# Tile 5's first layer by seven block products, a shorter x ring and another order of the work in a fused attention and MLP kernel

## The chip, the cores and the metric

The kernel runs on one core of one Trainium2 chip. The metric is the device time of one execution in microseconds (us); a kernel's time is the median of its runs. Below, PE is TensorE (matrix products), PEld its weight loads, DVE is VectorE, ACT is ScalarE, POOL is GpSimd and SP is SyncE, which issues most transfers.

## What is computed

Eight batches of attention with eight heads, 576 rows and 64 columns per head, in a form without a score matrix, and behind it a two-layer network on all 4608 rows:

```python
q_s = softmax(q, over the 64 columns)
k_s = softmax(k, over the 576 rows)
kv  = einsum('bhsd,bhse->bhde', k_s, v)
x   = einsum('bhsd,bhde->bhse', q_s, kv)     # becomes 4608 rows of 512
h   = x @ w_in                               # 512 -> 2048
g   = maximum(0.01 * h, h)
out = g @ w_out                              # 2048 -> 512
```

Inputs and output are 32-bit floats; the products are made of bf16 operands with 32-bit sums.

## The kernel before

**Attention, by batch.** `load` (line 76) brings q, k or v of one batch into one of six buffers of the pool `raw` (line 61), 1152 KB each. For k, the maximum over the rows is taken by a tree on DVE (`k_tree`, line 147: nine row groups, first four against four, then two against two, one against one, and the ninth), carried across partitions (`k_allmax`, line 162), subtracted (`k_sub`) and exponentiated on ACT (`k_exp`). For q, DVE takes maxima (`q_max`, line 222), POOL subtracts them, ACT exponentiates, DVE sums (`q_sum`) and normalises (`q_norm`), all in place of the loaded buffer or in `qe`. `q_turn` (line 454) sends the normalised q through a transposing transfer issued by SP; its result is `qX`. For batches 1 and 2 this is done in two halves, of five and of four row groups. PE makes k^T v (`kv_half`, line 288) and, in `quads` (line 433), x transposed in PSUM, named `po`; `move` (line 427) copies it into `xT`, a ring of columns (token) with the four blocks of 128 features. The ring has `NX = 4 * S` = 2304 columns (line 54).

**The network, by tile.** 4608 tokens are nine tiles of 512. In tile 0 both layers are plain. From tile 1 on the second layer is made by seven block products of a 2x2 block scheme instead of eight (`behind`, line 930, words "P"): sums and differences of g are made on DVE (line 1008, words "n") and those of w_out beforehand (`wsums`). The first layer comes in two forms:

- plain (`layer1`, line 511, words "u"): for each of the 16 feature blocks four products of 512 columns into one PSUM bank, then a leaky eviction on ACT (line 525, words "l");
- by seven block products (`ahead`, line 902, words "m"): for one quarter of the features 7 x 4 products of 256 columns; three partial sums per quarter are copied out by ACT (line 985, words "s1", "s5", "s6") into `part_spare`, three sums are made by DVE (line 989, by `total`, line 900, words "c11", "c22", "c12"), and four leaky evictions follow, three of which read from `part_spare`. It needs sums of x (`xsums`, words "X") and of w_in (`fsums`, words "F"), and buffers for partial sums, which are taken from the pool `raw` (words "Z").

Tiles 1 to 4 have the plain form, tiles 6, 7 and 8 the block form, and tile 5 the plain form for three quarters of the features and the block form for the fourth.

**What sets the order.** Each engine works through its own instructions in program order. Up to tile 0 that order is given by calls and by hooks (`at`). From tile 1 to the end of tile 6 it is the list of words `SCORE` (line 803); for tiles 7 and 8 it is `WEAVE` (line 845). A word issues all instructions of one step on whatever engines it uses. A digit ahead is the tile; "u13" is the second half's feature block 3. Of the words without a tile, "lq3" loads q of batch 3 (SP), "kt3.0" to "kt3.3" are steps of the tree, "km3" the maximum across partitions, "qm3" q's row maximum, "qt2.0" and "qt2.1" the transposing transfers, "A2.0" to "A2.2" the quads, "x2.01" a move on ACT. "d11" to "d22" add a kept partial sum (words "q1", "q5", "q6") to a PSUM bank into the output buffer (line 1027) and thereby empty that bank, "w" issues the stores.

Of the kernel before, what the change touches and what calls it, by code (L numbers as in the profile page):

```python
# [8 lines left out]
FP32 = mybir.dt.float32  # L9
# [16 lines left out]
def kernel(  # L26
# [9 lines left out]
    nc = tc.nc  # L36
# [3 lines left out]
    B, H, S, D = q.shape  # L40
# [22 lines left out]
    qe_pool = ctx.enter_context(tc.tile_pool(name="qe", bufs=1))  # L63
    mx_pool = ctx.enter_context(tc.tile_pool(name="mx", bufs=1))
# [82 lines left out]
    def k_tree(b, hs, steps=slice(0, 4)):  # L147
        n = hs.stop - hs.start
        ks = st[b]["k"][:, hs]
        if steps.start == 0:  # L150
            st[b]["t4"] = mx_pool.tile([P, HL, 4, D], FP32, name="t4")[:, 0:n]
        t4 = st[b]["t4"]
        t2, t1 = t4[:, :, 0:2], t4[:, :, 0]
        for o, i0, i1 in (
            (t4, ks[:, :, 0:4], ks[:, :, 4:8]),
            (t2, t2, t4[:, :, 2:4]),
            (t1, t1, t4[:, :, 1]),
            (st[b]["kmax"][:, hs], t1, ks[:, :, 8]),
        )[steps]:
            nc.vector.tensor_tensor(out=o, in0=i0, in1=i1, op=ALU.max)  # L160

# [265 lines left out]
    def move(eng, o, i):  # L427
        if eng is nc.scalar:
            eng.copy(out=o, in_=i)  # L429
        else:  # L430
            eng.tensor_copy(out=o, in_=i)
# [14 lines left out]
    def attend(b, gg, c0, n, engs, pool=psB_pool, tag=BANK_TAG):  # L446

        ps = [pool.tile([P, n], FP32, name="po", tag=tag) for _ in range(2)]
        qT = st[b]["qT", gg]
        quads(b, gg, ps, lambda hh: qT[:, hh].rearrange("c r l -> c (r l)")[:, c0 : c0 + n])  # L450
        for hp in range(2):
            move(engs[hp], xT[:, 2 * gg + hp, b % 4 * S + c0 : b % 4 * S + c0 + n], ps[hp])

    def q_turn(b, rs=ALLR):
        if "qX" not in st[b]:
# [3 lines left out]
            in_=st[b]["qe"][:, rs].rearrange("p r h d -> p (r h d)"),  # L459
        )  # L460

    def attend_made(b, i, g0, per):
        qX = st[b]["qX"].rearrange("c (r g) (h l) -> c g h r l", g=2, h=2)
        rs = XR[i]
        n = (rs.stop - rs.start) * L
        cols = slice(b % 4 * S + rs.start * L, b % 4 * S + rs.stop * L)
# [9 lines left out]
        return [(xT[:, 2 * g0 + hp : 2 * g0 + hp + 2 * per - 1 : 2, cols], ps[hp]) for hp in range(2)]  # L476

    def attend_joint(b, i):
        qX = st[b]["qX"].rearrange("c (r g) (h l) -> c g h r l", g=2, h=2)
# [7 lines left out]
        for gg in ggs:  # L487
# [7 lines left out]
        c0 = b % 4 * S + rs.start * L  # L495
        g0 = ggs[0]
        return [
            (xT[:, 2 * g0 + hp : 2 * ggs[-1] + hp + 1 : 2, c0 : c0 + n], ps[hp]) for hp in range(2)
        ]

    def attend_x(b, parts, engs):

        made = []
        for i in parts:
            per = 512 // ((XR[i].stop - XR[i].start) * L)
            for g0 in range(0, 2, per):
# [283 lines left out]
    def xsums(t, steps=slice(0, 4)):  # L790
# [10 lines left out]
            nc.vector.tensor_tensor(out=o, in0=x, in1=y, op=op)  # L801

    SCORE = """
        1u13 1u02 kt2.1 kt2.2 kt2.3 1u00 qm2.1 qm2.0 lq3 1u03 1l02 1l03 1l13 1l00 1u01 1u06 1u04 1l01 1u17
        qs2.1 qe2.1 1l06 km2 1l04 qu2.1 qs2.0 1l17 1u05 qe2.0 ks2 1u10 qu2.0 1u07 qn2.0 1P100 1l05 1u11 1l10
        lk3 qt2.0 1u12 1u16 va2 1l11 1l07 1u14 ksB2 1l16 1u15 1P101 1P110 1l12 1n0_0 1P200 1l14 1l15 1P201
        1P210 1P211 1P111 1n0_1 qn2.1 1n1_1 1P500 1P501 vb2 ke2 1q1 1P510 1n1_0 1d11 kv2 1P511 1q5 kr2 kd2
        1P600 1P601 1P610 1P611 qt2.1 1n3_0 lq4 1n3_1 1n2_1 1P300 lv3 1n2_0 1P301 A2.0 A2.1 A2.2 1q6 x2.01
        T3 kt3.0 kt3.1 x2.11 kt3.2 1P310 1P311 kt3.3 qm3 x2.20 1P700 1P701 1P710 1P711 x2.21 x2.00 x2.10
        2u11 2u00 2l00 2u01 2l01 2l11 2u10 2l10 va3 2u04 1d22 1P400 1P401 1P410 1P411 vb3 1d12 qm4 2u05 2l04  # L810
        qs3 qe3 2u14 2l14 2u02 2u06 2u12 lk5 2l05 2u13 2l02 2l06 2l12 km3 2u07 2u16 2u03 qu3 qn3 2l07 2l13
        2u17 1q21 2l03 2u15 2l15 2P100 ks3 ksB3 2n0_0 2l17 qs4 2P101 2P110 2P111 2P200 2l16 2P201 2P210
        2P211 2P500 2n0_1 2n1_0 2n1_1 2P501 2P510 lk4 kt4.0 lq5 ke3 kv3 kr3 2q1 2d11 2n2_0 1w0 2P600 qt3
        2P601 lv6 2P610 2P611 2P511 kd3 A3.0 kt4.1 2n2_1 2n3_0 kt4.2 2n3_1 A3.1 2q6 kt4.3 2q5 A3.2 2P700
        2P701 2P710 x3.01 2P711 x3.11 2d22 x3.10 2P300 x3.20 2P301 2P310 x3.21 qe4 km4 ks4 ksB4 kt5.0 lv4
        2P311 x3.00 2P400 va4 2P401 2P410 kt5.1 3u02 3l02 2P411 3u03 3u00 vb4 3l00 kt5.2 kt5.3 3u01 3l01 km5
        3l03 ke4 3u11 3l11 3u06 3u04 3l04 3u16 2q21 3l06 3l16 3u12 3l12 3u14 3u10 3l10 lk6 ks5 qu4 3u15 3l15
        kv4 3l14 kr4 kd4 3u07 2d12 qn4 3u05 3u13 3u17 3P100 3l05 3l07 3P101 3P110 3P111 lk7 3l13 3n0_0 3P500
        lv5 3l17 3n0_1 3P501 3P510 3q1 ke5 3n1_0 3n1_1 3n3_0 3P511 3P600 3n3_1 3q5 3P601 va5 3P610 3P611 3q6
        1w1 3P300 3P301 3P310 vb5 3P311 kt6.0 3n2_0 qt4 A4.0 A4.1 A4.2 kv5 x4.01 kt6.1 3n2_1 x4.00 x4.21  # L820
        x4.10 2w0 va6 3P700 kt6.2 kt6.3 3P701 3P710 qm5 qs5 3P711 3P200 3P201 x4.11 3P210 3P211 x4.20 kr5
        kd5 3d22 vb6 4u02 4l02 3P400 3P401 3d11 3P410 4u04 4u00 qe5 4l00 3P411 km6 4l04 4u05 4l05 3q21 4u03
        4u14 4l14 4l03 4u10 4l10 4u06 lv7 4u07 4u11 4l11 4u01 4l01 4l06 3d12 4l07 qu5 qn5 ks6 kt7.0 3w0 4u12
        4l12 4u13 F3 4l13 F1 4P100 4P101 4P110 F2 ke6 4u15 4P111 4q1 4n0_0 4l15 4u17 4l17 kt7.1 4n1_0 4u16
        3w1 4P500 4l16 4n0_1 4n2_0 qt5 A5.0 A5.1 x5.01 x5.10 x5.00 A5.2 kv6 x5.20 kt7.2 2w1 x5.11 4P501
        4P510 4n1_1 4P511 4q5 x5.21 4n3_0 4P600 4n3_1 4P200 4P601 4P610 4n2_1 X5.0 4P300 4P611 lq6 X5.1 X5.2
        4P201 4P301 4P310 4q6 X5.3 4P700 4P701 5u00 va7 kt7.3 4P210 F4 vb7 4P710 4P711 qm6 qs6 4d22 lq7 kr6
        4P211 4d11 5u04 4P311 kd6 4P400 4P401 5l00 4P410 5u02 km7 4P411 5l04 5u05 4q21 5l05 5l02 qm7 qe6 qu6
        5u15 5l15 5u11 5l11 ks7 Z0 5u03 5m5_3 5u12 5m1_3 5s1_3 5m2_3 5c11_3 qs7 4d12 5u01 5l12 5l03 5m6_3
        5u10 5s5_3 5m3_3 5s6_3 5c12_3 5l11_3 5m7_3 5u13 5l01 5P100 5P101 5c22_3 5l22_3 5m4_3 5l10 5l13 5u14  # L830
# [208 lines left out]
    def of_batch(word):  # L1039
# [108 lines left out]
```

## Time and profile before

| what | value |
|---|---|
| median of 3 runs | 267.45 us (267.39 to 267.73) |
| span of the profiled execution, first to last instruction | 265.6 us |
| difference of the two | 1.85 us |
| bytes read, written | 36.70 MB, 9.44 MB |
| SP's hardware queue | 32976 packets, 36.64 MB |

The profiled execution is one more than the three runs, and the profile gives its span alone as its own time; what lies outside the span is taken as the difference to the median. Busy time counts the time in which at least one instruction of an engine is at work. Products on PE are pipelined: one of 256 columns is listed with 273 ns but a new one starts every 109 ns, so prices are read from the length of a run of them. A landing time is the time from the issue of a transfer to its completion.

### The profile page before, as it was taken

Reading aid. Unit: us, or ns where it says so; the run is one execution under the profiler, and the core shown is the slowest. Engines: PE = TensorE matmul, PEld = TensorE weight load, DVE = VectorE, ACT = ScalarE, POOL = GpSimd, SP = SyncE. Lnnn points to the kernel's source line nnn. Section 1 sums busy time; section 2 is a strip of 40 time slices with the busy share of each in tenths; the row PEclk is TensorE's granted clock in tenths of the full one; section 3 lists DMA queues with packets and bytes.
Section 4 is the critical chain, followed back from the end, with each engine's and each line's share of the span. In section 5 each row is a group of like instructions: output and inputs, shape, how many; then the busy total and the mean of one; then the engine's idle time right before and its main releaser. Section 6 shows DMA issues by size and latency. Waiting matters only on the chain.

```text
span 265.6 us, 6314 instructions
## 1 busy us (share of the span) xinstructions
PE 255.3 (96%) x2570; PEld 190.0 (72%) x2582; DVE 223.2 (84%) x365; ACT 193.6 (73%) x370; POOL 62.5 (24%) x45
## 2 busy tenths in 40 slices
PE   8689999999999999999999999999999999999993
PEld 3267754457865687458988876688888888888882
DVE  2997999799998999989889897894998579779952
ACT  3977893699659769978887747887996489618930
POOL 2485451160038000250670019800000000000000
PEclk9999999999999999999999999999999999999999
DMA  6999999999899694858557725040383060032004
GB/s 239 344 211 357 317 211 275 326 309 306 247 399 304 145 316 156 284 223 169 181 127 156 226 67 173 20 91 4 81 174 74 21 139 2 0 93 68 1 2 158
DMA packets 37645, 46.48 MB, mean 175 GB/s; under 512 B 18160, under 2 KB 21232, under 8 KB 37616
## 3 DMA queue, kind: packets, MB, share of 16 engines
q1 hardware_dynamic: 32976, 36.64, 48.4%
q0 software_dynamic: 4320, 8.91, 13.4%
q10 hardware_dynamic: 320, 0.52, 0.6%
q8 instruction: 20, 0.33, 0.5%
q14 instruction: 9, 0.07, 0.1%
HBM read 36.70 MB, written 9.44 MB: 174 GB/s over the span
## 4 chain that ended last, share of the span: by engine, by line
PE 80%; DMA 7%; DVE 5%; POOL 1%; issue 1%
PE acc L951 37%; PE ph L516 24%; PE ph L921 15%; DMA q_raw<-in_q_dram 4%; DMA qX<-qe 3%; PE po L438 2%; DVE qmax L225 1%; PE pkv L294 1%; PE po L294 1%; DVE k_raw L380 1%; PE pout L541 1%; DVE k_raw L193 1%; POOL k_raw L83 1%; DVE qsum L273 1%; DVE qe L280 1%
## 5 line engine op out<-in xcount | busy, mean ns | idle before, releaser
L516 PE MATMUL ph<-xT,w_in_sb 128*128 128x256 bf16 (+3 forms) x488 | 83.6, 323 | 0.6
L525 ACT ACTIVATE gj<-ph 128x512 bf16<-128x512 f32 (+2 forms) x113 | 58.9, 575 | 14.1 <-PE ph L516 11.0
L516 PEld LDWEIGHTS <-w_in_sb 128*128 128x128 bf16 x496 | 48.1, 98 | 29.1 <-issue 0.6
L951 PEld LDWEIGHTS <-gs 128*128 128x128 bf16 x512 | 49.5, 98 | 6.5 <-issue 0.2
L256 POOL TENSOR_TENSOR q_raw<-q_raw,qmax 128x2304 f32<-128x2304 f32 (+3 forms) x10 | 29.7, 2975 | 63.8 <-DVE qmax L225 63.8
L951 PEld LDWEIGHTS <-gj 128*128 128x128 bf16 x384 | 37.4, 98 | 6.8 <-issue 0.5
L951 PE MATMUL acc<-w_out_sb,gj 128*128 128x256 bf16 x256 | 32.4, 273 | 0.0
L951 PE MATMUL acc<-wsum,gs 128*128 128x256 bf16 x256 | 30.8, 273 | 0.0
L951 PE MATMUL acc<-w_out_sb,gs 128*128 128x256 bf16 x256 | 30.6, 273 | 0.0
L900 DVE TENSOR_TENSOR part_spare<-ph,part_spare 128x512 f32<-128x512 f32 x39 | 25.5, 685 | 3.4 <-PE ph L921 2.8
L985 ACT COPY part_spare<-ph 128x512 f32<-128x512 f32 x39 | 21.5, 594 | 8.7 <-PE ph L921 8.4
L429 ACT CAST xT<-po 128x512 bf16<-128x512 f32 (+3 forms) x47 | 19.0, 488 | 7.9 <-PE po L438 7.8
L1008 DVE TENSOR_TENSOR gs<-gj 128x1024 bf16<-128x1024 bf16 (+1 forms) x40 | 22.3, 578 | 2.0 <-ACT gj L525 2.0
L273 DVE TENSOR_REDUCE qsum<-qe 128x36 f32<-128x2304 bf16 (+4 forms) x11 | 19.7, 1791 | 3.3 <-ACT qe L264 3.3
L921 PEld LDWEIGHTS <-fs_spare 128*128 128x128 bf16 x208 | 20.3, 98 | 3.0
L280 DVE TENSOR_TENSOR qe<-qe,qrec 128x2304 bf16<-128x2304 bf16 (+4 forms) x12 | 22.1, 1842 | 0.3
L1008 DVE TENSOR_TENSOR gs<-gj,gs 128x1024 bf16<-128x1024 bf16 (+1 forms) x40 | 22.1, 578 | 0.3
L1018 ACT COPY keep<-acc 128x512 f32<-128x512 f32 x22 | 12.8, 587 | 12.1 <-PE acc L951 12.0
L193 POOL TENSOR_TENSOR k_raw<-k_raw,kall 128x2304 f32<-128x2304 f32 x3 | 15.2, 5067 | 26.7 <-ACT gj L525 25.9
L900 DVE TENSOR_TENSOR out_sb<-acc,keep 128x512 f32<-128x512 f32 (+1 forms) x26 | 16.6, 644 | 5.4 <-issue 2.8
L921 PE MATMUL ph<-xs_spare,fs_spare 128*128 128x256 bf16 x156 | 20.9, 273 | 0.0
L225 DVE TENSOR_REDUCE qmax<-q_raw 128x36 f32<-128x2304 f32 (+4 forms) x11 | 19.6, 1793 | 0.5 <-DMA q_raw<-in_q_dram 0.5
(89 smaller groups left out, 322.5 us busy)
## 6 DMA issues: line engine op xcount, KB each, us to landing
out_dram<-out_sb SPq DMA_DIRECT2D x68, 128.0 KB, 2.4
q_raw<-in_q_dram SPq DMA_DIRECT2D x6, 1152.0 KB, 6.1
v_raw<-in_v_dram SPq DMA_DIRECT2D x6, 1152.0 KB, 7.2
k_raw<-in_k_dram SPq DMA_DIRECT2D x5, 1152.0 KB, 9.0
w_in_sb<-in_moe_w_in_dram POOLq DMA_DIRECT2D x4, 512.0 KB, 7.7
w_out_sb<-in_moe_w_out_dram POOLq DMA_DIRECT2D x3, 512.0 KB, 16.4
k_raw<-in_k_dram SPq DMA_DIRECT2D x2, 576.0 KB, 5.6
v_raw<-in_v_dram SPq DMA_DIRECT2D x2, 576.0 KB, 7.6
```

The costliest lines, as they stand in the source:

```text
L225: nc.vector.tensor_reduce(out=m, in_=st[b]["q"][:, :, rs], axis=AX.X, op=ALU.max)
L256: eng.tensor_tensor(out=qs, in0=qs, in1=st[b]["qmax", rs.start].unsqueeze(3).to_broadcast([P, HL, n, D]), op=ALU.subtract,)
L273: nc.vector.reduce_sum(out=qsum, in_=st[b]["qe"][:, rs], axis=AX.X)
L280: eng.tensor_tensor(out=qes, in0=qes, in1=st[b]["qrec", rs.start].unsqueeze(3).to_broadcast([P, n, HL, D]), op=ALU.mult,)
L429: eng.copy(out=o, in_=i)
L516: nc.tensor.matmul(ph[:, n0:n1], lhsT=w_in_sb[:, i, j * P : (j + 1) * P], rhs=xT[:, i, (c0 + n0) % NX : (c0 + n0) % NX + n1 - n0], start=( ...
L525: nc.scalar.activation(out=o, in_=ph, func=AF.Prelu, alpha=LEAKY_SLOPE)
L900: nc.vector.tensor_tensor(out=o, in0=x, in1=y, op=ALU.add)
L921: nc.tensor.matmul(bank[x, t, p][:, jj], lhsT=lhs(k, 2 * p + jj), rhs=rhs[:, k], start=(first and k == 0 and jj == 0), stop=(k == 1), skip ...
L951: nc.tensor.matmul(b[:, at_], lhsT=lhs(k)[:, sub * P : (sub + 1) * P], rhs=rhs[:, k], start=(first and k == 0 and at_ == 0), stop=(k % (NK ...
L985: nc.scalar.copy(out=fill(t, kind, p), in_=bank["Z" if kind == "s5" else "X", t, p])
L1008: nc.vector.tensor_tensor(out=o, in0=x, in1=y, op=ALU.subtract)
```

## The change

Tile 5's first layer takes the block form for all its quarters: the words "5u" and "5l" of three quarters (12 each) leave `SCORE`, and 21 words "5m", nine "5s", nine "5c" and twelve evictions "5l11" to "5l22" come in. The ring of x has 1280 columns for 2304; where a block of x crosses its end, `placed` returns two destinations and there are two moves. The tree takes three rows against three, then against the last three, and then one row at a time. The pool `raw` has seven buffers for six. And `SCORE` as a whole is another order of the words of tiles 1 to 6; `WEAVE` stays.

```diff
-    NX = 4 * S
+    NX = 20 * L
...
-    raw_pool = ctx.enter_context(tc.tile_pool(name="raw", bufs=6))
+    raw_pool = ctx.enter_context(tc.tile_pool(name="raw", bufs=7))
...
-            st[b]["t4"] = mx_pool.tile([P, HL, 4, D], FP32, name="t4")[:, 0:n]
-        t4 = st[b]["t4"]
-        t2, t1 = t4[:, :, 0:2], t4[:, :, 0]
+            st[b]["t3"] = mx_pool.tile([P, HL, 3, D], FP32, name="t3")[:, 0:n]
+        t3 = st[b]["t3"]
+        t1 = t3[:, :, 0]
         for o, i0, i1 in (
-            (t4, ks[:, :, 0:4], ks[:, :, 4:8]),
-            (t2, t2, t4[:, :, 2:4]),
-            (t1, t1, t4[:, :, 1]),
-            (st[b]["kmax"][:, hs], t1, ks[:, :, 8]),
+            (t3, ks[:, :, 0:3], ks[:, :, 3:6]),
+            (t3, t3, ks[:, :, 6:9]),
+            (t1, t1, t3[:, :, 1]),
+            (st[b]["kmax"][:, hs], t1, t3[:, :, 2]),
         )[steps]:
...
+    def placed(b, rs, blocks, ps):
+        r0, n = rs.start, rs.stop - rs.start
+        c0 = (b * S + r0 * L) % NX
+        cut = min(n * L, NX - c0)
+        parts = [(xT[:, blocks, c0 : c0 + cut], ps[:, :, 0:cut])]
+        if cut < n * L:
+            parts.append((xT[:, blocks, 0 : n * L - cut], ps[:, :, cut : n * L]))
+        return parts
...
-            move(nc.scalar, *st[b]["x", int(word[-2])][int(word[-1])])
+            for o, i in st[b]["x", int(word[-2])][int(word[-1])]:
+                move(nc.scalar, o, i)
```

Of `SCORE`, the stretch around batch 2's quads, before and after (the words between are left out):

```diff
-        lk3 qt2.0 ... qt2.1 1n3_0 lq4 1n3_1 1n2_1 1P300 lv3 1n2_0 1P301 A2.0 A2.1 A2.2 1q6 x2.01
-        T3 kt3.0 kt3.1 x2.11 kt3.2 1P310 1P311 kt3.3 qm3 x2.20 1P700 1P701 1P710 1P711 x2.21 x2.00 x2.10
-        2u11 2u00 2l00 2u01 2l01 2l11 2u10 2l10 va3 2u04 1d22 1P400 1P401 1P410 1P411 vb3 1d12 qm4
+        lk3 ... lq4 qt2.1 ksB2 ... lk4 ... 1q5 1P300 kd2 1d11 1n2_0 qt2.0 A2.0 A2.1 A2.2 1n3_1 1P611 1P310
+        lq3 x2.00 kt3.0 1P311 1n2_1 lv3 kt3.1 x2.20 1P301 kt3.2 1q6 1P700 1P710 x2.01 1P711 1P701 x2.21 lk5
+        x2.10 x2.11 2u01 2u00 2l00 va3 2u13 qm3 qs3 kt3.3 2u11 2l11 1d22 2u02 1P410 2u15 1P400
```

and the stretch of tile 5's first layer, after:

```diff
+        4d22 5m1_1 5m5_0 5s1_1 5m1_0 kd6 5s1_0 4P400 4P401 4P410 4P411 4q21 4P300 5m6_0 km7 qm7 4P200 5m2_0
+        4P201 4P310 5m6_1 4P311 5m5_1 5m1_2 5c11_0 qe6 qu6 ks7 5m2_1 5s6_1 5m7_1 5c11_1 5s6_0 5m7_0 2w1 5s5_1
...
+        5P110 5P111 5m3_3 5c12_3 4w1 5q1 qs7 qt6 5l21_2 5m7_3 5c22_3 5P200 5l12_3 5l22_3 5P500 5P510 5m4_3
```

More of the change, by code (lines that the diff above doesn't have):

```diff
@@ L451, in attend @@
         for hp in range(2):
-            move(engs[hp], xT[:, 2 * gg + hp, b % 4 * S + c0 : b % 4 * S + c0 + n], ps[hp])
+            move(engs[hp], xT[:, 2 * gg + hp, c0 : c0 + n], ps[hp])
     def q_turn(b, rs=ALLR):
@@ L475, in attend_made @@
             )
-        return [(xT[:, 2 * g0 + hp : 2 * g0 + hp + 2 * per - 1 : 2, cols], ps[hp]) for hp in range(2)]
+        return [placed(b, rs, slice(2 * g0 + hp, 2 * g0 + hp + 2 * per - 1, 2), ps[hp]) for hp in range(2)]
     def attend_joint(b, i):
@@ L494, in attend_joint @@
             )
-        c0 = b % 4 * S + rs.start * L
         g0 = ggs[0]
-        return [
-            (xT[:, 2 * g0 + hp : 2 * ggs[-1] + hp + 1 : 2, c0 : c0 + n], ps[hp]) for hp in range(2)
-        ]
+        return [placed(b, rs, slice(2 * g0 + hp, 2 * ggs[-1] + hp + 1, 2), ps[hp]) for hp in range(2)]
     def attend_x(b, parts, engs):
@@ L507, in attend_x @@
                 made += attend_made(b, i, g0, per)
-        for i, (o, p) in enumerate(made):
-            move(engs[i % len(engs)], o, p)
+        for i, parts_ in enumerate(made):
+            for o, p in parts_:
+                move(engs[i % len(engs)], o, p)
     def layer1(j, ph, c0, n, part=slice(0, 4), first=True, last=True):
@@ L814 @@
[L814 to L818, printed above, removed]
@@ new lines @@
+        1l17 1u12 qu2.1 1u10 va2 1u05 1l05 1u15 1l15 ks2 1l12 qn2.1 1u07 lk3 qs2.0 qe2.0 1u14 1u03 1l10 lq4
+        qt2.1 ksB2 qu2.0 1u11 1l11 1u01 1l14 lk4 1l01 1u04 1P200 1P201 1l03 1n0_0 1P100 1P210 1l04 1l07 1P101
+        1P110 1n0_1 qn2.0 1P500 vb2 1P510 1n1_1 1P211 1P501 1n1_0 ke2 1P111 1P511 1q1 T3 kv2 1P600 1P601 kr2
+        1P610 1n3_0 1q5 1P300 kd2 1d11 1n2_0 qt2.0 A2.0 A2.1 A2.2 1n3_1 1P611 1P310 lq3 x2.00 kt3.0 1P311 1n2_1
+        lv3 kt3.1 x2.20 1P301 kt3.2 1q6 1P700 1P710 x2.01 1P711 1P701 x2.21 lk5 x2.10 x2.11 2u01 2u00 2l00 va3
@@ new lines @@
+        qs4 3u03 3l13 2n3_0 3u02 vb4 2P310 3u01 Z0 kt4.3 3l03 lv5 2n3_1 km4 2P711 kt5.0 qe4 ks4 kt5.1 ksB4 ke4
+        2P311 3u10 kt5.2 3l02 3u04 3u00 3u14 2d22 2P300 2P400 2P410 3l10 2P411 kt5.3 km5 kt6.0 ks5 lv6 2P301
+        2d12 lk7 qu4 2P401 3l00 qn4 3u11 3l14 3l11 3l04 3u05 3l05 2q21 3u12 3l12 3l01 3u07 3l07 3u06 3u17 3l17
+        3l06 3u15 3u16 3n0_0 3l15 kv4 qt4 3P200 3l16 3P100 3P110 3n0_1 kt6.1 3P111 3P101 ke5 3P500 3P510 3P511
+        2w0 kr4 kd4 3q1 3n1_0 3n1_1 3P501 va5 vb5 kt6.2 3n3_0 3P201 A4.0 lv7 3n3_1 kt6.3 x4.00 A4.1 3P610 3P210
@@ L843 @@
+        A7.0 x7.00 6l12_3 6n1_0 6P500 6P111 6P101 6q1 6P510 6m4_3 6l21_3 6m4_2 6P610 6P600 6n0_1 6P511 6l21_2
+        6n1_1 6n2_0 6n3_1 6P601 6P611 6q6 A7.1 A7.2 x7.01 x7.10 5w1 x7.20 6P501 6P700 6n2_1 6P710 6q5 6P211
+        6P711 6P701 6n3_0 6d22 6P300 6P201 6P310 6P311 6P410 6P301 6P411 6d12 x7.11 x7.21 X7.0 X7.1 X7.2 6P400
+        6P401 6d11 X7.3 6w0 6q21 6w1
     """.split()
```

60 lines of the change are left out of this document (26 added, 34 removed).

## The prediction

> **What bounds the kernel now.** I read the page's first two parts, then the table of stages, then the chain of work that ended last, then the groups by shape, then SP's queue. The page first.
>
> ```profile
> span 265.6 us, 6314 instructions
> PE 255.3 (96%) x2570; PEld 190.0 (72%) x2582; DVE 223.2 (84%) x365; ACT 193.6 (73%) x370; POOL 62.5 (24%) x45
> PEclk9999999999999999999999999999999999999999
> ```
>
> PE is busy for 96% of the span at full granted clock. DVE with 84% and ACT with 73% have room on average, but an average hides the stages. The table of busy time in ten-microsecond stages shows them:
>
> ```profile
> 40.00:50.00 10.00, 9.52 (x125) 4.36 (x125) 8.09 (x11) 3.99 (x11) 2.23 (x3) 1.00 1.18 273
> 70.00:80.00 10.00, 9.95 (x83) 6.71 (x82) 9.90 (x11) 6.44 (x14) 2.75 (x1) 1.00 1.04 391
> 110.00:120.00 10.00, 9.80 (x121) 5.47 (x122) 8.79 (x14) 8.08 (x18) 5.06 (x1) 1.00 0.60 202
> 170.00:180.00 10.00, 9.95 (x85) 8.19 (x85) 9.66 (x13) 7.36 (x12) 1.63 (x1) 1.00 0.31 61
> 190.00:200.00 10.00, 10.00 (x94) 8.96 (x92) 9.75 (x13) 9.91 (x20) 0.00 (x0) 1.00 0.85 185
> ```
>
> The columns after the length are PE, PEld, DVE, ACT and POOL. From 50 us on PE is never under 9.80 of 10; the ten-microsecond stages that the five rows stand for lose 0.05 each, one loses 0.20, most lose nothing. So after 50 us there is at most about half a microsecond of idle PE to win, and the time there is simply PE's work. Only less PE work, or a new stall, can move the end. The row 190 to 200 matters for later: it lies in tile 6, whose first layer is already all block products, and PE loses nothing there with DVE at 9.75 and ACT at 9.91.
>
> The chain confirms it, and gives the price of PE's work:
>
> ```profile
> 38.66 8.99 DMA qX<-qe
> 47.70 0.47 PE po L438 x8
> ...
> 71.23 0.61 PE po L438 x16
> ...
> 78.89 1.75 PE acc L951 x16
> ...
> 114.04 0.15 issue
> ...
> 158.44 0.86 PE ph L516 x4
> ...
> 187.20 10.04 PE ph L921 x92
> ...
> 261.12 0.42 DVE out_sb L900
> ```
>
> From 47.7 to 261.1 the chain is PE almost without a break. Four products of 512 columns (L516) take 0.86 us, so 0.215 each. Ninety-two block products of 256 columns (L921) take 10.04, so 0.109 each. Before 47.7 the chain hangs on batch 1's transposed q (qX); after 261.1 come one addition and the last stores, 4.5 us.
>
> The span is 265.6 and the median of the runs 267.45, so 1.85 us lie outside the span; I take those as unchanged and add the sum to 267.45.
>
> **The change part by part.**
>
> *First layer of tile 5.* Three of its four quarters leave the plain form. Removed: 12 "u" words, each 4 products of 512 columns, so 48 × 0.215 = 10.3 us. Added: 21 "m" words, each 4 products of 256 columns, so 84 × 0.109 = 9.2 us. Difference: **-1.15 us on PE** (10.32 - 9.16), all in the stretch where PE is the chain. Cutting a tile at the ring's end moves from tile 4 to tile 2 (token 2048 is now a whole fit, token 1024 is cut at 1280); such a tile has eight 256-column products for four of 512, 0.872 for 0.86, in one tile before and in one after: nothing.
>
> The Trainium skill speaks against this edit: "TensorE: Matmul & The Clock Gate", section Back-to-back issue gap, gives a sustained spacing of about 131 ns for 512 columns and 81 ns for 128. By it 48 × 0.131 = 6.3 us would be removed and, at an estimate of some 0.10 each, 8.4 added: 2 us lost. The trace does not agree: 0.215 against 0.109, in long runs, are the same price per column.
>
> *What tile 5 adds to ACT and DVE.* The shapes and means:
>
> ```profile
> L525 ACT ACTIVATE gj<-ph 128x512 bf16<-128x512 f32 x81 | 44.3, 604 | 11.7 <-PE ph L516 10.0 <-PE ph L921 1.2 <-PE acc L951 0.3
> L900 DVE TENSOR_TENSOR part_spare<-ph,part_spare 128x512 f32<-128x512 f32 x39 | 25.5, 685 | 3.4 <-PE ph L921 2.8
> L985 ACT COPY part_spare<-ph 128x512 f32<-128x512 f32 x39 | 21.5, 594 | 8.7 <-PE ph L921 8.4
> L525 ACT ACTIVATE gj<-part_spare 128x512 bf16<-128x512 f32 x31 | 18.3, 635 | 1.0 <-DVE part_spare L900 1.0
> L429 ACT CAST xT<-po 128x512 bf16<-128x512 f32 x19 | 10.6, 611 | 3.1 <-PE po L438 3.1
> L429 ACT CAST xT<-po 128x320 bf16<-128x320 f32 x18 | 6.8, 448 | 4.0 <-PE po L438 4.0
> L160 DVE TENSOR_TENSOR t<-k_raw 128x1024 f32<-128x1024 f32 x6 | 7.3, 1215 | 0.0
> L160 DVE TENSOR_TENSOR t<-t 128x512 f32<-128x512 f32 x6 | 4.1, 686 | 0.1
> L429 ACT CAST xT<-po 128x128 bf16<-128x128 f32 x6 | 1.6, 292 | 0.0
> ```
>
> Nine more copies of partial sums on ACT (9 × 0.594 = 5.3 us) and nine more sums on DVE (9 × 0.685 = 6.2 us). The leaky evictions stay twelve for twelve; nine of them now read from SBUF at 0.635 for 0.604, 0.3 us. None of it is on PE. Is it covered? In the new order the words from the first to the last "m" of tile 5 hold 28 "m" and 19 "P" words, 47 × 4 × 0.109 = 20.5 us of PE. ACT has 12 copies (7.1), 14 evictions (about 8.7) and the exponentials, scalings and keeps of batch 7 and tile 4 (about 4.6): 20.4. DVE has 11 sums (7.5) and about 12 us of maxima, sums and products: some 19.9. These are sums of means; neighbours on an engine overlap, so the true load is below. That is as full as the stage 190 to 200, and there PE lost nothing. I cost it at 0; without the cover it would be at most the 0.5 us by which such a stage could overflow.
>
> *Ring of 1280 tokens.* Batches 2, 4 and 6 now cross the end of the ring, each in its first large block, so 3 × 4 moves become 24. A 512-column move split in two costs about 0.75 for 0.61, a 320-column one about 0.63 for 0.45 (estimates between the rows of 512, 320 and 128 columns): 12 × about 0.16 = 1.9 us on ACT, beside PE. The ring also makes the moves of a batch wait for the layer-1 reads of about two tiles back. These words stand ahead of the moves in PE's own order in every batch, so they are done: 0.
>
> *Three-row tree.* Elements per batch: 1024 + 512 + 256 + 256 before, 768 + 768 + 256 + 256 after. Halfway between the rows of 1024 and 512 a step of 768 costs 0.95, and 2 × 0.95 = 1.90 = 1.215 + 0.686. Nothing, in the head too, where the halves sum alike.
>
> *Seventh load buffer.* It moves transfers.
>
> ```profile
> 26.66 0.75 POOL L83 DMA_DIRECT2D k_raw<-in_k_dram x1 [1.13 <-ACT gj L525]
> ```
>
> Batch 2's k is issued up to 1.1 us earlier, since its buffer is new; it stands in POOL's DMA queue behind v of batch 1 and the weights either way. Bounds: qX of batch 1, which PE waits for at 47.7, lands at most 0.48 earlier in effect (PE's whole idle time in the stage 40 to 50), or 1.1 later if k crowds it. I take 0, the nearest to the row.
>
> *The new order.* Here I look only at what stands close to PE. SP issues nearly all transfers through one queue:
>
> ```profile
> 55.76 0.53 SPq L83 DMA_DIRECT2D q_raw<-in_q_dram  x1
> 56.39 0.50 SPq L83 DMA_DIRECT2D k_raw<-in_k_dram  x1
> 62.49 4.72 SPq L457 DMA_TRANSPOSE qX<-qe  x2
> 67.31 0.52 SPq L83 DMA_DIRECT2D q_raw<-in_q_dram  x1
> ```
>
> Their landings, from the views of q_raw, k_raw and qX in those windows:
>
> ```profile
> DMA to landing us min/median/max: 6.6/6.6/6.6
> ```
> ```profile
> DMA to landing us min/median/max: 9.0/9.0/9.0
> ```
> ```profile
> DMA to landing us min/median/max: 3.1/3.5/3.9
> ```
>
> So q of batch 3 landed at 62.3, k at 65.4 (3.0 later, one load's transfer time), the first half of qX at 66.4 and the second, issued about 66.0 with nothing ahead, at 69.1: 2.1 us before PE took it up at 71.23. In the new order SP has k3, q4, half of qX, **k of batch 4**, the other half, then q of batch 3. One more load stands between the halves. And batch 2's products come two "P" words earlier (16 instead of 18 are ahead), 2 × 0.44 = 0.87: PE is there at 70.4. If transfers leave the queue in order: q4 at 65.4, the first half at 66.4, k4 at 69.4, the second half 1.1 to 2 us later, 70.5 to 71.4. PE waits 0.1 to 1.0; if the half passes beside the load, 0. I take **+0.4**.
>
> The Trainium skill, "DMA: Bandwidth & Descriptors", section Queues, rings and completion order, says that SP owns one ring on each DMA engine and that descriptors are consumed in ring order; by that the wait is the upper end. The landings above agree with it.
>
> Two more changes between 128-row and 64-row products come with the new order (the quads of batches 4 and 7 are split); the chain's pieces of "issue" there are 0.05 to 0.15: +0.1 together.
>
> Sum: -1.15 + 0.4 + 0.1 = -0.65, so **266.8 us**.
>
> **The rivals.**
>
> *The load of q moves too far (slower).* q of batch 3 now sits in the place that issued at 67.31. Its reader is the row maximum of batch 3, and behind that on DVE, in order, stand the last tree step (0.42) and the sum that empties tile 1's bank, which PE's next "P4" overwrites. Before:
>
> ```profile
> 74.58 2.54 DVE L225 TENSOR_REDUCE qmax<-q_raw 128x36 f32<-128x2304 f32 x1
> 77.04 1.28 DVE L900 TENSOR_TENSOR out_sb<-acc,keep 128x512 f32<-128x512 f32 x2
> ```
>
> PE came to that word at 78.89 and, with the same words ahead of it, does so again. The load must land by 78.89 - 2.54 - 0.42 - 0.68 = 75.2. In the old order the load of that place took 7.2 us:
>
> ```profile
> DMA to landing us min/median/max: 7.2/7.2/7.2
> ```
>
> which gives 74.5. Beyond 75.2 every microsecond goes one to one into PE. If one more load than I count is ahead of it (3.0 us), it lands at 77.5 and costs 2.3: 267.45 - 1.05 + 2.3 = 268.7. For it: 0.7 us of slack and a fuller ring. Against: a wait at qX moves PE's word later too. Chance 0.16.
>
> *The wait takes the gain back (no change).* qX's second half at the late end, 1.0, and the later halves of batches 3, 4 and 7, which also come closer to PE, cost some 0.3 more: -1.15 + 0.1 + 1.3 = +0.25, 267.2 to 267.9. For it: the qX landings reach from 3.1 to 9.0 us over the run. Chance 0.27.
>
> ```profile
> DMA to landing us min/median/max: 3.1/4.6/9.0
> ```
>
> *No new wait at all.* Then -1.05, and up to 0.3 of the old idle pieces: 266.1 to 266.4. Chance 0.12.
>
> *Short products pay their weight loads*, so the edit itself loses. Every product comes with a weight load of its own:
>
> ```profile
> L921 PEld LDWEIGHTS <-fs_spare 128*128 128x128 bf16 x208 | 20.3, 98 | 3.0
> ```
>
> If the 36 extra loads were not hidden they would cost 36 × 0.098 = 3.5: 267.45 - 1.15 + 3.5 + 0.1 = 269.9. The 92 products in 10.04 us, with 0.109 each for 256 columns against 0.215 for 512, show them hidden; 0.01. (The rule cited above would come out on this side.)
>
> **How the numbers follow.** Forecast case, a wait of 0.1 to 0.8 at qX and nothing else: 266.5 to 267.1, chance 0.44. A measurement of this kernel can tell about 0.2%, 0.53 us, from no change: faster means under 266.92. Of the forecast case some 0.33 lies there and 0.11 within; with the case of no wait that makes faster 0.45. Within: 0.11 + 0.24 of the second rival = 0.35. Slower: 0.16 + 0.01 + 0.03 of the second rival = 0.20. The range reaches from the case of no wait, 266.1, to the middle of the slow rival, 268.4.
>
> **What would show it.** Right: 448 instead of 364 products in the "ahead" line and 48 fewer of 512 columns; PE at 9.9 to 10 in every stage from 50 to 260; PE's wait for qX grows from 0.3 to 0.7 or so, at about 70 us; the stage of tile 5 (about 165 to 190) shows DVE and ACT above 9 and PE at 10. The slow rival would show PE idle between 75 and 80 with DVE's row maximum as what ended it, and DVE itself waiting for the load of q. Wrong altogether would be PE losing time inside tile 5, or qX of batch 1 landing at another time than 47.7.

## The result and the profile after

| | median | runs | lowest to highest |
|---|---|---|---|
| before | 267.53 us | 7 | 267.39 to 268.44 |
| after | 268.96 us | 7 | 268.84 to 271.03 |

The ratio after to before is 1.0073, with an interval of 1.0049 to 1.0098. The change makes the kernel slower by about 1.4 us at the median, where 0.65 us faster was forecast. The profiled execution of the changed kernel took 270.19 us, 1.2 us more than the median; its trace tells where the loss is, and its size there is that of this execution.

The head of the page after:

```profile
span 268.4 us, 6431 instructions
PE 255.4 (95%) x2618; PEld 193.1 (72%) x2618; DVE 227.2 (85%) x374; ACT 200.0 (75%) x391; POOL 64.0 (24%) x45
```

PE's busy time is what it was (255.4 for 255.3), but the span is 2.8 us longer: the loss is idle PE. (The saving does not show in busy time: a product is listed with 0.16 us more than its spacing, so that much of every pause counts as busy.) Which stage? The table of ten-microsecond stages after, columns as before:

```profile
60.00:70.00 10.00, 9.86 (x146) 7.41 (x144) 9.96 (x15) 8.97 (x16) 0.00 (x0) 1.00 1.09 332
70.00:80.00 10.00, 7.00 (x73) 6.02 (x74) 8.05 (x11) 3.73 (x14) 0.87 (x1) 1.00 1.09 367
100.00:110.00 10.00, 9.69 (x78) 6.15 (x76) 9.82 (x21) 8.41 (x13) 0.00 (x0) 1.00 0.95 322
160.00:170.00 10.00, 10.00 (x94) 8.98 (x92) 9.70 (x15) 8.47 (x15) 10.00 (x3) 1.00 0.37 85
170.00:180.00 10.00, 10.00 (x94) 8.95 (x93) 9.06 (x12) 9.42 (x19) 1.02 (x1) 1.00 0.34 28
```

One stage carries nearly all of it: from 70 to 80 us PE is busy 7.00 of 10, before it was 9.95. Tile 5's stage, 160 to 180, is full at 10.00 with DVE and ACT above 9 part of the time, as forecast. The waits of PE, and the chain of work that ended last, name the cause:

```profile
PE po L438 <- DMA qX<-qe: 3.3, 2, 3.0
```
```profile
62.51 4.41 PE acc L959 x41
66.92 6.63 DMA qX<-qe
74.28 3.60 PE acc L959 x32
...
94.51 6.26 DMA qX<-qe
```

The wait (total, times, longest) is 3.3 us, 3.0 of it in front of batch 2's quads. The chain leaves PE at 66.92, when SP issues the second half of batch 2's qX, and comes back 6.63 us later. SP's queue shows what stands ahead of that half:

```profile
56.75 0.53 SPq L83 DMA_DIRECT2D k_raw<-in_k_dram  x1
57.40 0.50 SPq L83 DMA_DIRECT2D q_raw<-in_q_dram  x1
61.48 1.71 SPq L457 DMA_TRANSPOSE qX<-qe  x1
63.29 0.85 SPq L83 DMA_DIRECT2D k_raw<-in_k_dram  x1
66.92 1.43 SPq L457 DMA_TRANSPOSE qX<-qe  x1
```

This is the order that the prediction read from the words: k3, q4, half, k4, half. The landings of q4, of the first half, of k4 and of the second half, each from the view of its tile around its issue:

```profile
DMA to landing us min/median/max: 9.3/9.3/9.3
```
```profile
DMA to landing us min/median/max: 6.1/6.1/6.1
```
```profile
DMA to landing us min/median/max: 7.6/7.6/7.6
```
```profile
DMA to landing us min/median/max: 6.6/6.6/6.6
```

That is 66.7, 67.6, 70.9 and 73.5: strictly in the order of issue. PE was there at 70.6. Next to this everything else is small: between 55 and 105 us the start times of PE's products show another 0.28 us at 69.6, 0.35 at 58.8 and 61.2 together, and 0.38 at 100.3 for batch 3's qX; against that PE waits 0.15 at 47 for 0.48 before. With 3.07 at 70.3 by the same measure the account is 3.07 + 0.28 + 0.35 + 0.38 - 0.33, less the 1.15 of work, plus 0.1 for array changes: 2.7 of the 2.8 us.

### The profile page after: what moved, and what is told of

It reads as the page before. It is cut to its first block, busy times and chain, and to the rows that moved or that the text cites. A ratio compares the mean times of both kernels' runs of the same rounds, so it can differ in the third digit from the quotient of the medians.

```text
span 268.4 us, 6431 instructions
## 1 busy us (share of the span) xinstructions
PE 255.4 (95%) x2618; PEld 193.1 (72%) x2618; DVE 227.2 (85%) x374; ACT 200.0 (75%) x391; POOL 64.0 (24%) x45
## 4 chain that ended last, share of the span: by engine, by line
PE 84%; DMA 10%; DVE 3%; ACT 1%; issue 1%; POOL 0%; SPq 0%; POOLq 0%
PE acc L959 34%; PE ph L523 23%; PE ph L929 18%; PE pout L548 5%; DMA qX<-qe 5%; DMA w_in_sb<-in_moe_w_in_dram 3%; PE po L438 2%; DMA k_raw<-in_k_dram 2%; DVE t L160 1%; DVE k_raw L380 1%; ACT gj L532 1%; PE po L294 1%; PE pkv L294 1%; DVE kmax L160 0%; SPq L83 0%
## 5 line engine op out<-in xcount | busy, mean ns | idle before, releaser
L523 PE MATMUL ph<-xT,w_in_sb 128*128 128x256 bf16 (+3 forms) x448 | 72.8, 318 | 0.2 <-DMA w_in_sb<-in_moe_w_in_dram 0.2
L532 ACT ACTIVATE gj<-ph 128x512 bf16<-128x512 f32 (+2 forms) x104 | 54.3, 571 | 13.5 <-PE ph L523 8.6
L523 PEld LDWEIGHTS <-w_in_sb 128*128 128x128 bf16 x448 | 43.5, 98 | 25.5 <-issue 1.2
L993 ACT COPY part_spare<-ph 128x512 f32<-128x512 f32 x48 | 26.4, 592 | 9.9 <-PE ph L929 9.5
L908 DVE TENSOR_TENSOR part_spare<-ph,part_spare 128x512 f32<-128x512 f32 x48 | 31.3, 684 | 2.4 <-PE ph L929 1.7
L959 PE MATMUL acc<-w_out_sb,gs 128*128 128x256 bf16 x256 | 32.2, 273 | 0.1
L929 PEld LDWEIGHTS <-fs_spare 128*128 128x128 bf16 x256 | 25.1, 98 | 2.9
L929 PE MATMUL ph<-xs_spare,fs_spare 128*128 128x256 bf16 x192 | 26.2, 273 | 0.0
L429 ACT CAST xT<-po 128x320 bf16<-128x320 f32 (+5 forms) x59 | 20.2, 436 | 7.4 <-PE po L438 7.2
L532 ACT ACTIVATE gj<-part_spare 128x512 bf16<-128x512 f32 x40 | 23.5, 628 | 1.2 <-DVE part_spare L908 1.1
```

Of the source, the lines that this page charges most:

```text
L523: nc.tensor.matmul(ph[:, n0:n1], lhsT=w_in_sb[:, i, j * P : (j + 1) * P], rhs=xT[:, i, (c0 + n0) % NX : (c0 + n0) % NX + n1 - n0], start=( ...
L532: nc.scalar.activation(out=o, in_=ph, func=AF.Prelu, alpha=LEAKY_SLOPE)
L908: nc.vector.tensor_tensor(out=o, in0=x, in1=y, op=ALU.add)
L929: nc.tensor.matmul(bank[x, t, p][:, jj], lhsT=lhs(k, 2 * p + jj), rhs=rhs[:, k], start=(first and k == 0 and jj == 0), stop=(k == 1), skip ...
L959: nc.tensor.matmul(b[:, at_], lhsT=lhs(k)[:, sub * P : (sub + 1) * P], rhs=rhs[:, k], start=(first and k == 0 and at_ == 0), stop=(k % (NK ...
L993: nc.scalar.copy(out=fill(t, kind, p), in_=bank["Z" if kind == "s5" else "X", t, p])
```

## The experiments

**Is it k4 between the halves?** Only the load of batch 4's k is moved, to behind v3, outside the two halves:

```diff
- 1l11 1u01 1l14 lk4 1l01 1u04 ... 1n2_1 lv3 kt3.1
+ 1l11 1u01 1l14 1l01 1u04 ... 1n2_1 lv3 lk4 kt3.1
```

> The changed kernel with one word moved: the load of batch 4's k is issued behind q and v of batch 3 instead of between the two halves of batch 2's qX. Theory R (the ring: qX's second half stands behind k4 in SP's queue, and PE waits for it at about 70 us): the second half is issued at about 66.5 and lands 3.1 to 4.6 later, PE waits 0 to 0.6 there instead of 3.0, the time falls by 1.5 to 2.5 from 268.96 to 266.5 to 267.4. Rival P (the new order brings PE to batch 2's products 0.9 us too early, and DVE and ACT are late in any case, in tile 5 too): the wait stays above 2 us and the time stays within 0.4 of 268.96.

Measured: 267.40 us (266.97 to 267.91, 11 runs), ratio to the kernel before 0.9989 (0.9980 to 0.9998). PE's wait for qX moved to another batch:

```profile
PE po L438 <- DMA qX<-qe: 1.2, 1, 1.2
```
```profile
70.00:80.00 10.00, 10.00 (x103) 8.61 (x102) 8.84 (x12) 5.48 (x15) 2.11 (x1) 1.00 1.03 378
80.00:90.00 10.00, 9.98 (x92) 8.80 (x91) 9.52 (x14) 9.36 (x15) 6.01 (x2) 1.00 0.56 209
90.00:100.00 10.00, 8.77 (x156) 7.37 (x155) 10.00 (x17) 7.34 (x14) 0.00 (x0) 1.00 0.62 122
```

The second half now lands 3.4 us after its issue and the stage 70 to 80 is full. One word in a list of many hundreds was the loss. The time stands at the upper edge of the range of theory R. What is left is 1.2 us at 97 us, for batch 3's qX: SP issues it at 92.2 in this order, and issued it at 89.1 in the kernel before.

**Two loads between the halves.** lq3, too, is put between them:

```diff
- lk4 1l01 ... 1n3_1 1P611 1P310 lq3 x2.00
+ lk4 lq3 1l01 ... 1n3_1 1P611 1P310 x2.00
```

> The changed kernel with one more load, q of batch 3, moved ahead of qX's second half: two loads stand between the halves. Theory R: each load costs one transfer time, 3.0 us, so PE's wait for qX grows from 3.0 to about 6 and the time from 268.96 to 271.5 to 272. Rival P: nothing grows, 268.5 to 269.4; q of batch 3 comes earlier, which can only help the row maximum.

Measured: 274.66 us, ratio 1.0255 (1.0233 to 1.0278). PE, in order of time, and the stage:

```profile
75.81 1.18 PE L438 MATMUL po<-qX,kd 64*64 64x320 bf16 x16 [5.56 <-DMA qX<-qe]
76.92 1.04 PE L960 MATMUL acc<-wsum,gs 128*128 128x256 bf16 x4
```
```profile
70.00:80.00 10.00, 4.44 (x38) 3.10 (x36) 7.03 (x9) 3.08 (x11) 2.68 (x1) 0.66 1.13 326
```

The half landed 9.2 us after its issue, 2.6 more than with one load, and PE waited 5.6. Each load ahead in the queue shifts the half by about one load's transfer time. The time is 2.7 us beyond the range of theory R, and the clock accounts for most of that: 0.66 was granted in this stage, four products take 1.04 us of listed time for 0.60 elsewhere, and half a clock for the 3.4 us from the end of the pause to 79.2 costs about 1.7.

**k4 behind both halves, ahead of q3.** The load stays early, and batch 3's q is the one that comes behind it:

```diff
- 1l14 lk4 1l01 ... qt2.0 A2.0
+ 1l14 1l01 ... qt2.0 lk4 A2.0
```

> The changed kernel with k4 issued directly behind qX's second half, ahead of q of batch 3. Theory R: PE's wait for qX goes as in the run with k4 behind v, but q of batch 3 lands 3.0 us later, at about 77 to 79, past the 75.2 from which the row maximum holds up PE's next P4 of tile 1: PE waits 1 to 2 us at about 78 and DVE's wait for q grows by as much; time 267.5 to 268.7. If the slow rival of the prediction were not real, the time would be that of the run with k4 behind v, within 0.3.

Measured: 270.83 us, ratio 1.0118 (1.0103 to 1.0134). No wait for qX2, but these, of PE and of DVE, and DVE's row:

```profile
DVE qmax L225 <- DMA q_raw<-in_q_dram: 3.8, 1, 3.8
...
PE acc L960 <- DVE out_sb L909: 2.3, 1, 2.3
```
```profile
77.50 2.55 DVE L225 TENSOR_REDUCE qmax<-q_raw 128x36 f32<-128x2304 f32 x1 [3.76 <-DMA q_raw<-in_q_dram]
```

This is the prediction's slow rival, taken apart from the rest: q of batch 3 landed at 77.5, DVE's row maximum started there, the sum that empties tile 1's bank came behind it, and PE lost 2.3 us. The time is above the 267.5 to 268.7 that were expected: the clock fell here too, to 0.83 in the stage from 80 to 90 (last section). So k4 has no harmless place at that time: between the halves it delays qX, ahead of lq3 it delays q.

**k4 through another queue.** Same word in the order, but issued by POOL, which comes to it 6 us earlier than SP did:

```diff
- load(src, b, f"{kind[1]}_raw", [(ALLH, ALLR)])
+ load(src, b, f"{kind[1]}_raw", [(ALLH, ALLR)], nc.gpsimd if word == "lk4" else nc.sync)
```

> The changed kernel with k4 issued by POOL, through POOL's own DMA queue, at about the same time as before or a little earlier. If the order in SP's ring makes qX late, the second half is free of k4 and lands 3.1 to 5 us after its issue, and the time is 266.5 to 267.6. If the shared bandwidth makes it late (the same bytes move on the same 16 engines ahead of it), the wait stays above 1.5 us and the time is 268.2 to 269.2.

Measured: 270.82 us (268.75 to 271.36, 4 runs), ratio 1.0099 (1.0065 to 1.0134). The median lies above both ranges that were expected. The trace is that of the run of 268.75 us; the other three took 270.76 to 271.36, with mean clocks of 0.990 to 0.992 for its 0.999, and have no trace. In the trace PE waits 2.0 us for qX2:

```profile
72.28 0.68 PE L438 MATMUL po<-qX,kd 64*64 64x320 bf16 x16 [2.03 <-DMA qX<-qe]
```

POOL issues k4 at 57.32; the load of q4 by SP:

```profile
L83 SPq DMA_DIRECT2D q_raw<-in_q_dram x1: 486/486/486, 56.3 to 56.3; - x1
...
DMA to landing us min/median/max: 12.4/12.4/12.4
```

q4, ahead of the halves in SP's queue, took 12.4 us for 9.3, and the halves come behind it. In this trace the transfers of two queues share what one queue had for itself: the bytes ahead count, and k4 in another queue still delays the halves. The Trainium skill, "DMA: Bandwidth & Descriptors", section Issuing engines are not separate DMA queues, states this: transfers run on the same 16 DMA engines and interleave, whoever started them. The trace agrees.

**PE later, k4 where the change put it.** The prediction gave two causes for the wait: k4, and quads that come two P words (0.87 us) earlier. Here the second is undone:

```diff
- qt2.0 A2.0 A2.1 A2.2 1n3_1 1P611 1P310 lq3
+ qt2.0 1P611 1P310 A2.0 A2.1 A2.2 1n3_1 lq3
```

> The changed kernel with two P words (0.87 us of PE work) moved from behind batch 2's products to ahead of them, where the old order had them; k4 stays between the halves of qX. Theory R: PE's wait for qX shrinks by that much, from 1.7 to 3.0 to 0.8 to 2.2, and the time by 0.6 to 0.9, to about 268.1, not to that of the kernel before. Rival P (the early place of these products is the whole cause): the wait goes below 0.5 and the time to 267.0 or less.

Measured: 269.11 us (267.53 to 269.94, 10 runs), ratio 1.0049 (1.0030 to 1.0069). The time did not fall as theory R said: the median is that of the change, the interval overlaps its interval, and the ten runs fall into two groups, four of 267.5 to 268.2 and six of 269.0 to 269.9. The trace (268.97 us) has two waits for a qX; the longest, 1.1, is batch 3's, and the one for qX2 is 0.95:

```profile
PE po L438 <- DMA qX<-qe: 2.0, 2, 1.1
```
```profile
72.11 0.68 PE L438 MATMUL po<-qX,kd 64*64 64x320 bf16 x16 [0.95 <-DMA qX<-qe]
```

k4 landed at 70.9 here too, but the half 1.2 us behind it, for 2.7 in the trace of the change: this last step varies from run to run. Of the 2.05 us by which the wait is shorter, 1.5 are the half's earlier landing and 0.6 is PE's later arrival (71.2 for 70.6). So the early quads are the smaller part of the wait and k4 the larger, as these two traces show it; in the times of the runs the quads' part doesn't show.

**Ring, tree and seventh buffer alone.** The change with the old list of words, tile 5 as before:

> The changed kernel with the old order of the words, and with it the old form of tile 5 (one quarter by block products); ring of 1280 columns, three-row tree and seven load buffers as in the changed kernel. Theory R (only the place of one load in SP's ring made the change slower): the ring, the tree and the seventh buffer cost nothing that can be measured, 267.3 to 268.0 beside 267.6 for the kernel before. Rival S (the shorter ring with its 12 extra moves, or the seventh buffer that lets loads run ahead, carries the loss): 268.3 or more.

Measured: 267.15 us against 267.50, ratio 0.9987 (0.9978 to 0.9996). These parts cost nothing; the time is below the range of theory R, and they give some 0.35 us (0.1 to 0.6 by the interval). No stage after 50 us has a new wait.

**Old start, new end.** The old order up to the middle of tile 3, then the new order with tile 5 in block form:

> The first 254 words of the old order (to the middle of tile 3, with qX of batches 2 and 3 and their products), then the rest in the new order, with all of tile 5's first layer by block products. Theory R: PE waits for qX of batches 2 and 3 as little as in the kernel before, and the 1.15 us of PE work that tile 5 saves comes through: 266.3 to 266.9 beside 267.6, with PE at 10.00 in tile 5's stage. Rival T (tile 5's extra 9 copies and 9 sums hold PE up, so the gain was never there): 267.4 or more.

Measured: 267.08 us, ratio 0.9987 (0.9979 to 0.9996): no better than without tile 5's new form, and between the ranges of the two theories. The waits of PE show a new one, in front of batch 4's quads:

```profile
PE po L438 <- ACT vb L211: 1.1, 1, 1.1
```

The releaser named here isn't the true one. The view of qX says that batch 4's transposing transfer was issued at 119.5 and took this long, and the quads start at 124.08:

```profile
DMA to landing us min/median/max: 4.6/4.6/4.6
```

With the old order the same transfer landed at 123.4 in the run above and at 125.0 in the kernel before, and the quads start at 125.5 in both. In the joined order PE comes to the quads 2.5 us earlier: six words of PE with 2.6 us of work fewer stand ahead of them.

**The same with batch 4's quads later:**

```diff
- 3P201 A4.0 lv7 3n3_1 kt6.3 x4.00 A4.1 3P610 3P210 3P611 3P600
+ 3P201 lv7 3n3_1 kt6.3 3P610 3P210 3P611 A4.0 x4.00 A4.1 3P600
```

> As the kernel with the old start and the new end (267.08 us, one new TensorE gap of 1.14 us at 122.7 us, in front of batch 4's quad products, whose qX was issued at 119.5 us and landed at 124.1 us), with those products (A4.0, A4.1) three products' words later in TensorE's order, behind 3P611: about 1.3 us. Theory 1 (the 7-product first layer is worth its 1.15 us of TensorE work, and each time it was eaten by a late qX): the gap goes and the time falls by 1.0 to 1.2 us, to 265.9-266.2 us, ratio about 0.994-0.995 to the kernel before. Theory 2 (other engines are so full from there on that the gain comes back as waits later in the program): the gap moves, and the time stays at 266.8-267.2 us.

Measured: 267.35 us against 267.70, ratio 0.9988 (0.9978 to 0.9997). Theory 1 fails for this kernel. The gap at 122.7 is gone: from batch 3's quads (98.49 here, 97.99 there) to batch 5's (148.02, 148.22) PE needs 0.70 us less. But the next stretch, with tile 5's first layer, to batch 6's quads (180.60, 180.16), takes 0.64 longer: five pieces of idle PE of 0.03 to 0.22 between 156 and 168, four of them from 164 on. ACT's row there in this kernel, then in the one before it:

```profile
160.27 2.12 ACT L264 ACTIVATE qe<-q_raw 128x2304 bf16<-128x2304 f32 x1 [1.00 <-POOL q_raw L256]
```
```profile
159.75 2.12 ACT L264 ACTIVATE qe<-q_raw 128x2304 bf16<-128x2304 f32 x1 [0.29 <-POOL q_raw L256]
```

ACT waits 0.7 us longer for POOL's subtraction for batch 6, and the copies and evictions of tile 5 queue behind it. POOL starts 0.56 us behind DVE's row maximum in both kernels, and DVE is late, here and there:

```profile
153.08 2.55 DVE L225 TENSOR_REDUCE qmax<-q_raw 128x36 f32<-128x2304 f32 x1
```
```profile
152.56 2.54 DVE L225 TENSOR_REDUCE qmax<-q_raw 128x36 f32<-128x2304 f32 x1
```

This trace runs 0.50 us behind the other from its start (batch 1's quads at 48.14 and 47.64). PE has made that up by batch 5's quads, 0.2 ahead, and DVE has not, 0.52 behind; from 136 us to this row DVE has no pause of 0.05 us in which to catch up. The two make the 0.7. So the engines beside PE have no room here, as theory 2 says, though its time is missed by 0.15: where PE alone comes 0.7 us earlier, it loses 0.64 in tile 5.

**That order with tile 5 plain again** (12 words "u" and "l" for 21 "m" with their evictions, in three quarters):

> The same order as the one before it in this call, but three of the four quarters of tile 5's first layer are plain products again, as in the kernel before (12 groups of four 512-column products in place of 21 groups of four 256-column products). Theory 1: 1.0 to 1.2 us slower than that one, 267.0-267.3 us, that is, tile 5's new form is worth 1.0-1.2 us where nothing waits. Theory 2: within 0.3 us of it.

In this kernel, and in the last one below, the plain evictions write whole rows of g's buffers, some of them before the last products of tile 4 have read what stood there, so tile 4's output is not the reference's; the products are the same in number and kind. Measured: 269.22 us, 1.87 above the kernel with the block form. But PE has a new gap of 0.85 us at 166.5, where it waits for an eviction, and one of 0.30 at 177.0, so this pair doesn't give the price.

**First mended version.** The first experiment's kernel, with batch 3's q normalised and sent ahead of k's subtractions on DVE:

```diff
- qu3 2u17 ks3 2l17 ksB3 qn3 qt3 2u05
+ qu3 2u17 2l17 qn3 qt3 ks3 ksB3 2u05
```

> The kernel with k4 behind v of batch 3 (267.4), and on DVE the normalising of q of batch 3 ahead of the two subtractions of k, so that qX of batch 3 is issued about 2.7 us earlier. Theory R: PE's wait for that qX, 1.2 us in the last profile, goes to 0; 266.4 to 266.9. If the subtractions, which now come later, hold up k's exponential and the products of batch 3, PE waits there instead and the time stays at 267.2 to 267.8.

Measured: 266.98 us against 267.50, ratio 0.9978 (0.9969 to 0.9987), between the two ranges. The wait for qX3 is gone; instead batch 3's k products wait 0.5 us for ACT's exponential, and batch 4's quads 0.35.

**Second mended version.** ks3 back ahead of qn3, only ksB3 behind qt3; batch 4's quads three words later, as above:

> As the kernel with k4 behind v3 and batch 3's q normalised first (266.98 us), with ks3 back ahead of q's normalisation (only the larger half of k's sums, ksB3, stays behind it), which should take away most of the 0.59 us gap at 93.65 us in front of batch 3's k products, and with batch 4's quad products three words later, which takes away the 0.26 us gap at 123.5 us. Theory 1: 266.1-266.5 us. Theory 2 (the gaps move on): 266.8-267.1 us. A third case: qX3's issue is later by the 1.2 us or so that ks3 takes on VectorE, and the products that wait for it lose 0.3-0.6 us: 266.6-267.0 us.

Measured: 266.66 us (266.51 to 267.51, 7 runs) against 267.70, ratio 0.9964 (0.9951 to 0.9977): about 1.0 us faster than the kernel before, the best version of this study. After batch 1's quads its trace shows no wait of PE of 0.25 us or more, and none in tile 5:

```profile
160.00:170.00 10.00, 10.00 (x94) 8.97 (x92) 9.76 (x15) 9.29 (x18) 7.66 (x2) 1.00 0.19 43
```

The time is in the range of the third case, but the waits of that case aren't there; theory 1's range is missed by 0.16.

**The second mended version with tile 5 plain**, the evictions close behind their products:

> The mended kernel (ratio 0.9964 to the kernel before) with three of tile 5's four quarters plain again: 12 groups of four 512-column products in place of 21 groups of four 256-column products, each eviction directly behind the next group, nothing else moved. Theory 1 (the block form is worth its 1.15 us of TensorE work wherever no load is waited for): 1.0 to 1.3 us slower than the mended kernel, ratio to the kernel before 0.9995 to 1.0015, and no TensorE gap over 0.3 us after 48 us. Theory 2 (the mended kernel wins by its order and its ring, and tile 5's form gives little): ratio 0.996 to 0.998.

Measured: 268.00 us against 267.76, ratio 1.0007 (0.9996 to 1.0018). The start of batch 6's quads (L438), first with tile 5 in block form, then plain:

```profile
179.09 0.69 PE L438 MATMUL po<-qX,kd 64*64 64x512 bf16 x16
```
```profile
180.28 0.69 PE L438 MATMUL po<-qX,kd 64*64 64x512 bf16 x16
```

In both kernels batch 5's quads start at 147.16. Between the two PE has no idle piece over 0.1 us in either. Tile 5's block form is worth 1.19 us of PE, as the prediction's first term says, and theory 1 holds.

## Why the prediction was wrong

**PE's saving of 1.15: right.** 1.19 by the last pair of traces, about 1.15 by the ratios 0.9964 and 1.0007 (give or take 0.5, by their intervals). With that the rival that short products pay their weight loads (269.9) is out, though the measured time lies on its side. The number of block products rose as forecast (448):

```profile
L929 PE MATMUL ph<-xs_spare,fs_spare 128*128 128x256 bf16 x192 | 26.2, 273 | 0.0
L929 PE MATMUL ph<-xT,w_in_sb 128*128 128x256 bf16 x128 | 17.4, 273 | 0.0
L929 PE MATMUL ph<-xT,fs_spare 128*128 128x256 bf16 x64 | 9.4, 273 | 0.0
L929 PE MATMUL ph<-xs_spare,w_in_sb 128*128 128x256 bf16 x64 | 9.1, 272 | 0.0
```

**ACT and DVE in tile 5, costed at 0: right** (PE 10.00 there). In the change PE comes to tile 5 late, which eases the stage; in the second mended version it does not, and PE is full there too. The price without the cover was near as well: 0.5 estimated, 0.64 met in the kernel with batch 4's quads later.

**Ring, tree, buffers, costed at 0: right**, some 0.35 us on the good side. Batch 1's qX, which the prediction wanted at 47.7, landed at 47.3 in the change and at 47.5 with these parts alone.

**The wait at qX2, +0.4: this is the step that failed.** The mechanism was named, with its place and its transfers; the term was mis-sized, 3.0 us in the trace. The prediction took "q4 at 65.4, the first half at 66.4, k4 at 69.4" from the one old trace. The new ones are 66.7, 67.6 and 70.9. SP issues k3 and q4 1.0 us later here, but that is not the whole cause: with the later quads SP issued them at the old times, and q4 landed at 66.7 all the same.

```profile
56.44 0.50 SPq L83 DMA_DIRECT2D q_raw<-in_q_dram  x1
```
```profile
DMA to landing us min/median/max: 10.2/10.2/10.2
```

Six traces have SP's new order up to q4 (the change, the first three experiments, the later quads, the first mended version): q4 landed between 65.7 and 67.1, in none as early as 65.4. What makes the spread stays open. And the prediction took 1.1 to 2 us for the half behind k4; it was 2.7 in this trace, 1.2 in that with later quads, and 1.2 behind the second load where two stood between the halves. Set into the prediction's own sum: 69.4 and 1.55, the middle of 1.1 to 2, against PE at 70.4 give 0.55, of which it took 0.4; 0.55 + 1.5 for k4's landing + 1.1 for the half - 0.2 for PE, which was there at 70.6, make 3.0. The upper end of the term, 1.0, had covered the spread of the last step alone, not that of the landings ahead of it.

The smaller waits of the changed kernel (0.28, 0.35 and 0.38, less 0.33 at batch 1) make 0.7 more that the sum did not hold; 0.3 of it stood in a rival.

For the median, without a trace of its own, the wait must be about 1.2 us shorter if that is where the runs differ; the two traces whose half landed 1.5 us closer to the load ahead make this likely and don't prove it.

**The rivals.** "The wait takes the gain back" described what happened, with a price of 1.3 in all where it was 3.3. The slow rival, q of batch 3, named a real mechanism: in the experiment that set it apart the load landed at 77.5 and cost 2.3 us, which are the two numbers that the prediction gave for one more load ahead (the time was higher, by the clock). In the changed kernel itself q3, issued at 68.45, landed at 76.4, beyond the limit of 75.2; it cost nothing there, since PE was 3.0 us late by then. So both waits sat in the order, one behind the other, and taking away only the first could have uncovered the second; moving k4 behind v3 took away both. "No new wait at all" (266.1 to 266.4) is nearly what the second mended version, with another order, comes to: 0.9964 of 267.45 is 266.5.

**Two more array changes, +0.1:** not set apart. With tile 5 plain the mended order stands at 1.0007 to the kernel before, in which this and the parts costed at 0 are together.

## What to carry to other kernels

Where one queue carries nearly all transfers and is full, a landing in a new order is worked out from the landing of the transfer ahead of it, all the way from the first transfer whose place changed, and the term's upper end has to hold the spread of every landing on the way: 1.4 us for q4 here, in six traces of the same order. A small transfer that PE needs next doesn't belong behind a load that nobody needs for long, and another queue did not help it here. Work taken off the engine that bounds a kernel brings every later deadline forward by as much: before counting the gain, list the transfers whose slack is smaller than the gain, as batch 2's, 3's and 4's qX were here.

## What the runs showed of the hardware

A pause of PE can go with a stretch at half clock, as in two of these traces. With the pause of 5.56 us the granted clock of the stage was 0.66. The half clock set in during the pause, and from its end to 79.2 us a 256-column product started every 213 ns for 109. With the one of 2.3 us, which ended at 81.04, the clock was 0.83 in the stage from 80 to 90; the products started every 213 ns from 81.9 to 85.3 us, so the half clock set in 0.9 us behind the pause, and cost some 1.7 us. The stages, first of the longer pause, then of the shorter:

```profile
73.00:76.00 3.00, 0.19 (x4) 0.18 (x7) 2.51 (x3) 0.00 (x0) 0.00 (x0) 0.50 1.27 189
76.00:79.00 3.00, 3.00 (x26) 1.97 (x19) 1.52 (x2) 2.08 (x7) 1.68 (x1) 0.50 1.06 393
```
```profile
80.00:90.00 10.00, 8.96 (x67) 7.32 (x67) 9.52 (x16) 7.92 (x11) 8.12 (x2) 0.83 0.48 179
82.00:85.00 3.00, 3.00 (x16) 2.07 (x15) 2.93 (x4) 2.92 (x5) 3.00 (x2) 0.50 0.90 329
```

After the pause of 3.0 us in the profiled execution of the change it stayed at 1.00. Two of its other runs, 270.76 and 271.03 us, have mean clocks of 0.992 and 0.993, as three of the runs with k4 through POOL have 0.990 to 0.992, so some of these executions may have paid this too; no trace of them is there. The Trainium skill, "TensorE: Matmul & The Clock Gate", section HAM oscillation, names idle gaps over some 3.4 us as the limit; here 2.3 us were enough once and 3.0 were not another time, which a limit in the length of the pause alone doesn't give. The page's Part 1 says that the window watched is free-running, which would let the same pause fall either way; no run here separates that.
